# Attention backward at one query row: half of O by wide matmuls with a DRAM scratch, and sum p·dp on VectorE

## The chip, the cores and the metric

One core of one Trainium2 chip. The time is device time in microseconds (us) of one execution, and the figures are medians of several executions. The span in the profile is about 2 us shorter than the time (644.5 for 646.47 us in the profiled run of the kernel before), because it runs from the first to the last instruction.

## The reference

The reference computes softmax attention with one query row per head, and its gradients. There are 32 heads, 8192 keys and head size 128, all in bf16.

```python
scores = jnp.einsum('bhqd,bhkd->bhqk', q, k) * 128 ** -0.5     # q: 1,32,1,128   k, v: 1,32,8192,128
attn   = softmax(scores)
out    = jnp.einsum('bhqk,bhkd->bhqd', attn, v)                # out_0 = O
# out_1, out_2, out_3 = the gradients of q, k, v for grad_out (vjp)
```

For each head with p = softmax, dO = grad_out and dp = V·dO, the outputs are dV = p ⊗ dO and ds = p·(dp − sum p·dp)·scale, and from it dK = ds ⊗ q and dQ = ds·K. The sum of p·dp over the keys equals O·dO, so a kernel may take either. For each head 2 MiB each of K and V are read, and 2 MiB each of dK and dV are written: 268 MB in all.

## The kernel before

A head goes through these stages: K is transposed by blocks on VectorE, TensorE makes the scores from it, then comes the softmax. V is transposed on TensorE (32 fp32 transposes, four groups of eight). O is 64 matmuls with one moving column, each with 128 rows of V as its weights. dp comes from the transposed V, and dV and dK are outer products on VectorE. K has three buffers, V, dV and dK two each.

```python
    def contract(Xt, rep, out_col, first=0, last=NT):        # O: 64 matmuls of one column
        for n in range(first, last):
            nc.tensor.matmul(out_col, lhsT=Xt[:, n, :], rhs=rep[:, n, 0:1],
                             start=(n == 0), stop=(n == NT - 1), skip_group_check=True)
    # ... (cut) in the loop over heads, after the softmax:
        v_transposes(h, 0)
        v_transposes(h, 1)
        v_transposes(h, 2)
        contract(Vt[h], x["p"], x["m"][:, 2:3])
        nc.scalar.copy(o_all[:, h:h + 1], x["m"][:, 2:3])
        v_scores(h, 0)                                       # dp
        v_scores(h, 1)
        v_transposes(h, 3)
        nc.tensor.matmul(x["m"][:, 1:2], lhsT=do_f[:, h:h + 1].to_broadcast([P, P]),   # O.dO
                         rhs=o_all[:, h:h + 1], start=True, stop=True, skip_group_check=True)
        v_scores(h, 2)
        v_scores(h, 3)
        # ... (cut) four outer products dV, the store of dV, the load of V two heads on;
        # dK and dQ of a head follow in the next head's turn
```

## Time and profile before

| before | |
|---|---|
| time | 646.4 us (646.16 to 646.51, 3 runs) |
| DMA in mid-run | all 16 engines busy, 428 GB/s |
| TensorE, VectorE, ScalarE busy | 75%, 78%, 28% |
| mean granted TensorE clock (share of full speed that TensorE was allowed) | 0.60 |

Three more lines are wanted. The first is the page's busy times. The others are groups: busy time and mean ns of one, then idle time before them with what ended it.

```profile
PE 481.0 (75%) x9673; PEld 452.0 (70%) x9673; DVE 505.5 (78%) x653; ACT 183.5 (28%) x332; POOL 0.7 (0%) x6
...
L210 DVE TENSOR_TENSOR G_dv<-p_rep,qd 128x2048 bf16<-128x2048 bf16 x128 | 148.2, 1221 | 90.3 <-DMA out_dram<-G_dv 84.6
L183 PE MATMUL T_ps<-ident_f,Vt 128*128 128x128 f32 x1024 | 203.4, 382 | 0.2 <-PE m_ps L294 0.2
```

VectorE stands still for 84.6 us in all because an old dV has not been written out yet: compute waits for transfers. A V transpose is recorded with 382 ns on the mean of two granted clocks, 0.5 ("cold" below) and 1.0 ("warm"): it starts 213 ns after the one before at 0.5 and 109 ns after it at 1.0 (medians of this trace). The records of neighbours overlap, as their busy time of 203.4 us for 1024 (199 ns each) shows.

### The profile page before, as it was taken

To read this page: it belongs to the slowest core of one execution; us is meant where nothing else is said; L and a number is where in the kernel's file an instruction comes from. 1 tells how busy PE (TensorE), PEld (TensorE's weight loads), DVE (VectorE), ACT (ScalarE), POOL (GpSimd) and SP (SyncE) were. 2 spreads that over 40 slices of the span, in tenths; PEclk is the share of its full clock that TensorE was granted. 3 is DMA by queue.
4 is the path that set the end of the run, shared out by engine and by line. 5 is a ranking of instruction groups with operands and counts; after the bars stand their busy time and mean duration, and the time that the engine had idled before them with its cause. 6 is when DMAs were issued, how large, how long until landed. Compare 5 with 4: busy or idle time off the path is not lost.

```text
span 644.5 us, 20935 instructions
## 1 busy us (share of the span) xinstructions
PE 481.0 (75%) x9673; PEld 452.0 (70%) x9673; DVE 505.5 (78%) x653; ACT 183.5 (28%) x332; POOL 0.7 (0%) x6
## 2 busy tenths in 40 slices
PE   3898888886677877768777787667786777877780
PEld 2888888886677866768666777667785676866670
DVE  5989899867977779777788777797767977778860
ACT  2333333332233222233222332223322223222230
POOL 0000000000000000000000000000000000000000
PEclk9766666655666655666556666556655666655665
DMA  8999999999999999999999999999999999999985
GB/s 349 407 425 430 424 425 423 429 426 431 427 428 427 427 427 429 429 429 425 433 422 433 425 430 427 427 429 425 427 429 425 431 425 429 429 427 430 424 365 238
DMA packets 19718, 269.80 MB, mean 419 GB/s; under 512 B 2352, under 2 KB 2352, under 8 KB 2864
## 3 DMA queue, kind: packets, MB, share of 16 engines
q1 hardware_dynamic: 19584, 268.47, 98.2%
q8 instruction: 75, 1.23, 0.7%
q14 instruction: 11, 0.09, 0.0%
q10 hardware_dynamic: 48, 0.01, 0.0%
HBM read 134.23 MB, written 134.23 MB: 417 GB/s over the span
## 4 chain that ended last, share of the span: by engine, by line
DMA 59%; PE 21%; DVE 14%; ACT 2%; issue 1%; SPq 0%; DVEq 0%; ACTq 0%
DMA Kt<-in_k_dram 48%; DVE XK_sb L146 8%; PE T_ps L183 8%; DMA out_dram<-G_dv 5%; DMA out_dram<-G_dk 5%; PE s_ps L157 5%; DVE G_dk L210 4%; PE dp_ps L200 3%; PE m_ps L200 2%; PE dp_ps L195 2%; ACT XT_sb L185 1%; PE m_ps L294 1%; DVE G_dv L210 1%; PE s_ps L173 1%; DVE sm L163 1%
## 5 line engine op out<-in xcount | busy, mean ns | idle before, releaser
L210 DVE TENSOR_TENSOR G_dv<-p_rep,qd 128x2048 bf16<-128x2048 bf16 x128 | 148.2, 1221 | 90.3 <-DMA out_dram<-G_dv 84.6
L183 PE MATMUL T_ps<-ident_f,Vt 128*128 128x128 f32 x1024 | 203.4, 382 | 0.2 <-PE m_ps L294 0.2
L183 PEld LDWEIGHTS T_ps<-ident_f,Vt 128*128 128x128 f32 x1024 | 190.7, 210 | 0.2 <-issue 0.2
L185 ACT COPY XT_sb<-T_ps 128x1024 f32<-128x1024 f32 x128 | 128.6, 1013 | 129.3 <-PE T_ps L183 127.2
L210 DVE TENSOR_TENSOR G_dk<-ds_rep,qd 128x2048 bf16<-128x2048 bf16 x128 | 155.6, 1218 | 2.9 <-DMA out_dram<-G_dk 1.9
L146 DVE STREAM_TRANSPOSE XK_sb<-Kt 128x1024 f32<-128x1024 f32 x128 | 148.3, 1214 | 5.8 <-DMA Kt<-in_k_dram 4.7
L157 PEld LDWEIGHTS <-XK_sb 128*128 128x128 bf16 x2048 | 57.7, 104 | 90.7 <-DVE pdt L234 79.9
L157 PE MATMUL s_ps<-q_blk,XK_sb 128*128 128x4 bf16 x2048 | 59.7, 168 | 82.1 <-DVE pdt L234 72.1
L195 PE MATMUL dp_ps<-do_blk,XT_sb 128*128 128x2 bf16 x2048 | 66.7, 164 | 18.1 <-ACT XT_sb L185 18.1
L195 PEld LDWEIGHTS <-XT_sb 128*128 128x128 bf16 x2048 | 64.9, 102 | 20.7 <-ACT XT_sb L185 20.7
L200 PE MATMUL dp_ps<-ds_rep,Kt 128*128 128x1 bf16 x2048 | 64.1, 165 | 1.3 <-issue 1.0
L200 PEld LDWEIGHTS <-Kt 128*128 128x128 bf16 x2048 | 59.6, 104 | 6.8 <-issue 6.6
L244 ACT COPY dq_all<-dp_ps 128x1 f32<-128x1 f32 x32 | 5.1, 159 | 192.4 <-PE dp_ps L200 178.5
L200 PEld LDWEIGHTS <-Vt 128*128 128x128 bf16 x2048 | 57.7, 97 | 0.9
L200 PE MATMUL m_ps<-p_rep,Vt 128*128 128x1 bf16 x2048 | 56.9, 164 | 0.0
L294 PEld LDWEIGHTS m_ps<-rs,ones_f 128*128 128x128 f32 x64 | 16.0, 311 | 49.9 <-ACT e L293 49.9
L294 PE MATMUL m_ps<-rs,ones_f 128*128 128x1 f32 x64 | 18.8, 362 | 40.5 <-ACT e L293 40.5
L303 ACT ACTIVATE p_rep<-e,rinv 128x256 bf16<-128x256 f32 x32 | 16.3, 508 | 30.1 <-DVE rinv L301 30.1
L163 DVE TENSOR_TENSOR sm<-s_ps,in_quad 128x256 f32<-128x256 f32 x32 | 13.6, 424 | 11.1 <-PE s_ps L157 7.9
L229 ACT CAST qd<-s_ps 128x256 bf16<-128x256 f32 x32 | 11.9, 372 | 32.2 <-PE s_ps L225 32.2
L236 DVE SCALAR_TENSOR_TENSOR ds_rep<-dp_ps,pdt,p_s 128x256 bf16<-128x256 f32 x32 | 15.5, 484 | 5.2 <-PE dp_ps L195 2.4
L293 ACT ACTIVATE e<-s_ps,nbias 128x64 f32<-128x64 f32 x32 | 10.0, 313 | 31.8 <-DVE nbias L290 31.8
(44 smaller groups left out, 143.4 us busy)
## 6 DMA issues: line engine op xcount, KB each, us to landing
Vt<-in_v_dram SPq DMA_DIRECT2D x32, 2048.0 KB, 30.0
Kt<-in_k_dram SPq DMA_DIRECT2D x31, 2048.0 KB, 30.8
out_dram<-G_dv SPq DMA_DIRECT2D x30, 2048.0 KB, 34.6
out_dram<-G_dk SPq DMA_DIRECT2D x30, 2048.0 KB, 33.6
out_dram<-G_dv SPq DMA_DIRECT2D x4, 1024.0 KB, 15.0
out_dram<-G_dk SPq DMA_DIRECT2D x4, 1024.0 KB, 13.3
Kt<-in_k_dram SPq DMA_DIRECT2D x4, 512.0 KB, 5.1
out_dram<-fin_sb SPq DMA_DIRECT2D x2, 8.0 KB, 13.1
```

Source lines behind the costliest of these rows:

```text
L146: nc.vector.transpose(XK[h][:, :, :, u, :], slots(Kt[h], u, NCH).rearrange("p g d -> p (g d)").bitcast(F32).rearrange("p (g w j) -> p g w ...
L157: nc.tensor.matmul(out[:, g, :], lhsT=cols[:, g, c // 2, c % 2], rhs=q_blk[:, h, c, :], start=(c == 0), stop=(c == 2 * NB - 1), skip_group ...
L163: nc.vector.tensor_tensor(x["sm"][:], x["s"][:, 0:NT].rearrange("p (a g) -> p a g", a=NQ).unsqueeze(2) .to_broadcast([P, NQ, NCH, CH]), in ...
L183: nc.tensor.transpose(T_ps[:, i, :], words[:, m * P:(m + 1) * P], ident_f[:])
L185: nc.scalar.copy(X[:], T_ps[:])
L195: nc.tensor.matmul(st[h]["dp"][:, n:n + 2], lhsT=X[:, i, e2, :], rhs=do_blk[:, h, e2, :], start=(e2 == 0), stop=(e2 == 1), skip_group_chec ...
L200: nc.tensor.matmul(out_col, lhsT=Xt[:, n, :], rhs=rep[:, n, 0:1], start=(n == 0), stop=(n == NT - 1), skip_group_check=True)
L210: nc.vector.tensor_tensor(slots(G, r, 4).rearrange("p n (a b) -> p n a b", b=R), slots(rep, r, 4).unsqueeze(2).to_broadcast([P, Q, D // R, ...
L229: nc.scalar.copy(x["qd"][:].rearrange("p a d -> p (a d)"), x["s"][:, 256:512])
L236: nc.vector.scalar_tensor_tensor(out=x["ds"][:], in0=x["dp"][:, 0:NT].unsqueeze(2).to_broadcast([P, NT, R]), scalar=pdt[:], in1=x["p_s"][: ...
L294: nc.tensor.matmul(x["m"][:, 0:1], lhsT=ones_f[:], rhs=rs[:], start=True, stop=True, skip_group_check=True)
L303: nc.scalar.activation(x["p"][:], e[:].unsqueeze(2).to_broadcast([P, NT, R]), ACT.Copy, scale=rinv[:])
```

## The change

The intent is to take work off TensorE's longest stage. The first half of O is made by 8 matmuls whose *moving* operand is V, 512 columns (four rows of 128) wide, with four columns of p as weights. Of each 4x512 result only the four diagonal 1x128 blocks are wanted. The whole 8 KB go to a DRAM scratch. At the very end all diagonals are read back, summed, and added to the other half. Since O is then not known in time for O·dO, VectorE takes sum p·dp.

```diff
+    def o_wide(h):
+        for g in range(NT // 2 // R):
+            nc.tensor.matmul(x["s"][0:R, :], lhsT=x["p"][:, R * g:R * (g + 1), 0],
+                             rhs=Vt[h][:, R * g:R * (g + 1), :].rearrange("p n d -> p (n d)"),
+                             start=(g == 0), stop=(g == NT // 2 // R - 1), skip_group_check=True)
+        nc.scalar.copy(four[:], x["s"][0:R, :])
+        nc.sync.dma_start(scratch[h, 0:R * R * D].rearrange("(a c) -> a c", a=R), four[:])
+    def o_narrow(h):     # 32 one-column matmuls for the second half
+    def pd_of(h):
+        nc.vector.tensor_tensor_reduce(out=junk[:], in0=x["p_s"][:], in1=x["dp"][:, 0:NT], scale=1.0,
+                                       scalar=0.0, op0=ALU.mult, op1=ALU.add, accum_out=pd[:])
+        nc.tensor.matmul(x["m"][:, 1:2], lhsT=ones_s[:], rhs=pd[:], start=True, stop=True, ...)
 ... (cut) next head's turn, between the third and the fourth block of its K:
+        if h > 0:
+            pd_of(p_)
 ... (cut)
         v_transposes(h, 1)
+        o_wide(h)
         v_transposes(h, 2)
-        contract(Vt[h], x["p"], x["m"][:, 2:3])
-        nc.scalar.copy(o_all[:, h:h + 1], x["m"][:, 2:3])
+        o_narrow(h)
 ... (cut)
-        nc.tensor.matmul(x["m"][:, 1:2], lhsT=do_f[:, h:h + 1].to_broadcast([P, P]), rhs=o_all[:, h:h + 1], ...)
 ... (cut) last head, before the last dK:
-            result(o_all, out_0)
+            nc.sync.dma_start(blocks[:], scratch[:].rearrange("h (a c) -> h a c", a=R)[:, :, 0:D])
 ... (cut) after everything else:
+    nc.vector.reduce_sum(block_sum[:], blocks[:].rearrange("h a d -> h d a"), axis=AX.X)
+    nc.tensor.transpose(fin_ps[0:H, 0, :], o_all[:], ident_f[:])
+    nc.vector.tensor_tensor(o_sb[:], fin_ps[0:H, 0, :], block_sum[:], op=ALU.add)
+    nc.sync.dma_start(out_0.rearrange("b h s d -> (b h s) d"), o_sb[:])
```

More of the change, by code (lines that the diff above doesn't have):

```diff
@@ L54 @@
     small = ctx.enter_context(tc.tile_pool(name="small", bufs=2))
+    fours = ctx.enter_context(tc.tile_pool(name="fours", bufs=3))
+    dram = ctx.enter_context(tc.tile_pool(name="scr", bufs=1, space=bass.MemoryType.DRAM))
     psT = ctx.enter_context(tc.tile_pool(name="psT", bufs=2, space=PSUM))
@@ L122 @@
     twice = consts.tile([H, 2, 2, W], BF16)
-    do_f = consts.tile([P, H], F32)
     def do_columns():
@@ L131, in do_columns @@
             nc.tensor.transpose(tp[:, e2, 0:H], twice[:, e2].rearrange("h t j -> h (t j)"), ident[0:H, 0:H])
-        nc.tensor.transpose(tp[:, 2, 0:H], rows[:, 1, :], ident[0:H, 0:H])
         for e2 in range(2):
@@ L135, in do_columns @@
                 nc.scalar.copy(do_blk[t * W:(t + 1) * W, :, e2, t], tp[t * W:(t + 1) * W, e2, 0:H])
-        nc.scalar.copy(do_f[:], tp[:, 2, 0:H])
+    ones_s = consts.tile([P, P], F32)
+    nc.vector.memset(ones_s[:], 1.0 / scale)
+    scratch = dram.tile([H, R * (R + 1) * D], F32, name="scratch")
     o_all = consts.tile([P, H], F32)
@@ L201, in contract @@
                              start=(n == 0), stop=(n == NT - 1), skip_group_check=True)
+    def o_wide(h):
+        x = st[h]
+        for g in range(NT // 2 // R):
+            nc.tensor.matmul(x["s"][0:R, :], lhsT=x["p"][:, R * g:R * (g + 1), 0],
+                             rhs=Vt[h][:, R * g:R * (g + 1), :].rearrange("p n d -> p (n d)"),
+                             start=(g == 0), stop=(g == NT // 2 // R - 1), skip_group_check=True)
+        four = fours.tile([R, R * D], F32, tag="four", name="four")
+        nc.scalar.copy(four[:], x["s"][0:R, :])
+        nc.sync.dma_start(scratch[h, 0:R * R * D].rearrange("(a c) -> a c", a=R), four[:])
+    def o_narrow(h):
+        x = st[h]
+        for n in range(NT // 2, NT):
+            nc.tensor.matmul(x["m"][:, 2:3], lhsT=Vt[h][:, n, :], rhs=x["p"][:, n, 0:1],
+                             start=(n == NT // 2), stop=(n == NT - 1), skip_group_check=True)
+        nc.scalar.copy(o_all[:, h:h + 1], x["m"][:, 2:3])
+    def pd_of(h):
+        x = st[h]
+        junk = small.tile([P, NT], F32, tag="junk")
+        pd = small.tile([P, 1], F32, tag="pd")
+        nc.vector.tensor_tensor_reduce(out=junk[:], in0=x["p_s"][:], in1=x["dp"][:, 0:NT], scale=1.0,
+                                       scalar=0.0, op0=ALU.mult, op1=ALU.add, accum_out=pd[:])
+        nc.tensor.matmul(x["m"][:, 1:2], lhsT=ones_s[:], rhs=pd[:], start=True, stop=True, skip_group_check=True)
     def outer(h, which, r):
@@ L259 @@
             rows_bc(h)
-            for u in range(NCH):
+            for u in range(NCH - 1):
                 k_blocks(h, u)
+        if h > 0:
+            pd_of(p_)
+        if h < H:
+            k_blocks(h, NCH - 1)
             k_scores(h)
@@ L313 @@
         v_transposes(h, 3)
-        nc.tensor.matmul(x["m"][:, 1:2], lhsT=do_f[:, h:h + 1].to_broadcast([P, P]), rhs=o_all[:, h:h + 1],
-                         start=True, stop=True, skip_group_check=True)
         v_scores(h, 2)
@@ L326 @@
         if h == H - 1:
-            result(o_all, out_0)
+            blocks = consts.tile([H, R, D], F32)
+            nc.sync.dma_start(blocks[:], scratch[:].rearrange("h (a c) -> h a c", a=R)[:, :, 0:D])
     result(dq_all, out_1)
+    block_sum = consts.tile([H, D], F32)
+    nc.vector.reduce_sum(block_sum[:], blocks[:].rearrange("h a d -> h d a"), axis=AX.X)
+    fin_ps = psT.tile([P, CH // 2, P], F32, tag="T", name="fin_o")
+    nc.tensor.transpose(fin_ps[0:H, 0, :], o_all[:], ident_f[:])
+    o_sb = consts.tile([H, D], BF16)
+    nc.vector.tensor_tensor(o_sb[:], fin_ps[0:H, 0, :], block_sum[:], op=ALU.add)
+    nc.sync.dma_start(out_0.rearrange("b h s d -> (b h s) d"), o_sb[:])
     order.__exit__(None, None, None)
```

## The prediction

> **What bounds the kernel now.** I read the page from the top, then the transfers, then the chain of waits, then the timeline of two heads and of the end. First the busy slices and the rate.
>
> ```profile
> PEclk9766666655666655666556666556655666655665
> DMA  8999999999999999999999999999999999999985
> GB/s 349 407 425 430 424 425 423 429 426 431 427 428 427 427 427 429 429 429 425 433 422 433 425 430 427 427 429 425 427 429 425 431 425 429 429 427 430 424 365 238
> HBM read 134.23 MB, written 134.23 MB: 417 GB/s over the span
> ```
>
> The DMA row is full from the second slice to the last but two, at a rate that hardly moves (422 to 433 GB/s). TensorE, VectorE and ScalarE stand at 75%, 78% and 28%. The table of stretches says the same without rounding (its columns are the span of the stretch, the busy time of PE, PEld, DVE, ACT and POOL with their counts, the granted clock, the DMA share, GB/s):
>
> ```profile
> 200.00:300.00 100.00, 75.77 (x1519) 71.27 (x1519) 78.64 (x100) 28.55 (x51) 0.00 (x0) 0.59 1.01 428
> 500.00:600.00 100.00, 76.16 (x1552) 71.66 (x1551) 79.58 (x102) 28.97 (x51) 0.00 (x0) 0.59 1.01 428
> ```
>
> All 16 DMA engines are in use throughout. One head moves 4 x 2 MiB = 8.39 MB; at 428 GB/s that is 19.6 us. The chain of waits repeats with just this period:
>
> ```profile
> 234.50 30.84 DMA Kt<-in_k_dram
> 265.37 4.62 DVE XK_sb L146 x4
> 270.05 1.87 PE s_ps L157 x64
> 271.92 0.85 PE dp_ps L200 x32
> 272.77 0.37 PE s_ps L173 x8
> 273.14 0.94 PE dp_ps L200 x32
> 274.12 30.85 DMA Kt<-in_k_dram
> ```
>
> 274.12 - 234.50 = 39.62 us for two heads, 19.8 us for one. Compute is 8.8 us of it; a K tile is 30.8 us under way although 2 MiB need 4.9 us alone: some five other transfers stand ahead of it. That backlog is the slack, as a microsecond more of compute comes off the queueing, not onto the end.
>
> How close compute is to becoming the bound shows in the first 117 us, before the backlog is full: the chain there goes through compute alone, and its 24 transposes of V start at 32.89, 50.15, 67.63, 84.81 and 101.90: 17.25 us per head, 2.5 us under the transfers.
>
> The end decides what little can move:
>
> ```profile
> 626.00:630.00 4.00, 1.48 (x46) 1.21 (x43) 3.96 (x4) 0.63 (x3) 0.00 (x0) 0.50 0.80 337
> 630.00:634.00 4.00, 0.00 (x0) 0.00 (x0) 0.00 (x0) 0.00 (x0) 0.00 (x0) 0.50 0.95 398
> 634.00:638.00 4.00, 0.00 (x0) 0.00 (x0) 0.00 (x0) 0.00 (x0) 0.00 (x0) 0.50 0.57 239
> 638.00:642.00 4.00, 0.00 (x0) 0.00 (x0) 0.00 (x0) 0.00 (x0) 0.00 (x0) 0.50 0.36 152
> ```
>
> The last engine is done by 630; 12 us of writes follow, in the last 8 of which about half of the DMA engines are already idle. The packet records agree: about half finish near 634 us, the others at 640 to 643 us. So the end is the backlog of the laggards. They had some 10 us of older work when the first half of the last dK was issued at 627.7, since that dK takes them only 4.9 us. Why they lag I infer: the second line of the queues below is instruction fetch, 75 packets that share the data's engines. If they all land on eight engines, that is 75/8 x 0.61 us = 5.7 us on each, about the lag (16 KB packets take 0.61 us in the packet records).
>
> ```profile
> q1 hardware_dynamic: 19584, 268.47, 98.2%
> q8 instruction: 75, 1.23, 0.7%
> ```
>
> [...] 24 fp32 transposes take 4.7 to 5.4 us, about 0.21 us each at granted 0.5, and 8 take 0.86 us in the warm window. [...] the trace's mean of 0.59 would be 0.5 with about one window of 3.4 us in each 19.7 us.
>
> **The change part by part, per head.**
> *TensorE.* Out: 32 of the 64 V contractions (64 take 1.59 us in the chain, so -0.80) and the fp32 product of O and dO (-0.42, the two passes in the timeline). In: 8 matmuls of 512 columns, 1.7 us warm to 3.4 us cold; they follow 16 transposes that have already run 3.4 us, so I take two to four cold and the rest warm: 2.3 us. Also in: the sum of pd over the partitions, an fp32 column product of the same kind as the removed one, +0.42, but issued before the K scores, where TensorE idles (PE s_ps waited 72.1 us in all for VectorE). The last 8 transposes of V gain perhaps 0.4 us from the warmer clock. Sum: -0.80 - 0.42 + 2.3 + 0.42 - 0.4 = +1.1 us, and at worst (all cold, no gain) +2.6 us. Compute then needs 18.3 us per head, at worst 19.8, against 19.7 for the transfers. TensorE busy about 75 to 80%, mean clock 0.60 to about 0.65.
> *VectorE.* In: one reduction of 128x64 fp32 with a PSUM operand; the nearest rows are p_s (128x64, 255 ns) and mx (218 ns), so about 0.3 us with the readout of the sum. DVE has 15.8 us of work in 19.7 and waits 84.6 us in all for old dV writes: hidden.
> *ScalarE.* In: the copy of 4x512 out of PSUM. From 372 ns for 256 columns and 1013 ns for 1024 the slope is 0.83 ns, so 0.59 us, between copies that have slack (28% busy).
> *Transfers.* In: 8 KB of scratch per head and 64 KB read once: 0.33 MB of 268 MB, 0.1%. If the writes sit on four engines, each gets 2 KB per head: from 309 ns for 8 KB and 611 ns for 16 KB, 2 KB take about 0.083 us; with the semaphore write about 0.09; x 32 = 3 us on those four. If they are laggards, the end moves by 3 us; if they are of the half that is done 7 us early, by nothing. I give each half: +1.5.
> *Fewer instructions.* The build has 15,153 entries for TensorE in place of 16,660, some 190 more on the others: net some 1,300 fewer. At the fetched 1.23 MB over about 17,500 entries, 70 B each, that is 92 KB or 5.6 packets of 16 KB less: 5.6 / 8 x 0.61 = 0.4 us less on the laggards (an estimate, if eight engines do the fetching).
> *Window of transfers.* In the built order each transfer waits for the one eight before it, which shares its semaphore. A head now issues five, not four, so at most about 6.4 large ones are open where there were 6.3 to 7. I followed the order: dV of a head now waits for dK of two heads before (about 5 us later issue, landing order unchanged), the others hardly at all. Six open transfers still fill the engines: 0.
> *The end.* O's first result was written at 625.3, hidden. Now the blocks' read waits for the last scratch write, the sum comes after it, and one 8 KB write is issued last. The read stands behind the last dV, before the last dK, thus lands some 3 us before the end; sum, addition and issue fit in that or overrun: +0 to 1.5, I take +0.5. The last dK is ready about 2 us later (1.1 TensorE, 1 for pd, now serial), inside the 10 us of backlog: 0.
>
> Sum: 646.4 + 1.5 - 0.4 + 0.5 = 648.0 us.
>
> **The rivals.**
> *TensorE becomes the bound.* If the eight matmuls run cold and something adds half a microsecond, a head takes 20.3 us, and 32 x 0.5 = 16 us more: 662 us. For it: the clock, 0.5 most of the time, and only 2.5 us of distance. Against it: the warm window follows the V transposes in every head, and the 17.25 us itself held ready time on VectorE.
> *The serial end.* The blocks' read, the sum and one write after all else, each with its landing (the two small writes of before took 13.1 us behind the queue): if the last dK is held up in the issuing queue behind the wait for the last scratch write, and the read is slow, +3 to 6 us: 650 to 652.
> *Four engines hot.* All of the 3 us and a late last scratch write on laggards: 650.5.
> *Less TensorE work helps.* If the half of O and the product were on the path, -1.2 us x 32 = -38 us. The chain of waits and full DMA row speak against it: transfers alone are 627 us (268.47 MB at 428 GB/s).
>
> **Range and chances.** The floor is near 645 (less fetch, nothing else); the hot engines plus a clumsy end give 651 to 652. Range 645.0 to 652.0. 2% slower is 659.3, for which only the TensorE rival is enough: 3%. 2% faster is 633.5, at which the transfers leave 6 us for start and end: under 1%.
>
> **What would show it.** Right: DMA share 1.01 and 428 GB/s in the middle; K loads still about 30 us; a head still 19.8 us; clock up; new waits of the issuing queue on transfers, without gaps in the DMA row; the scratch writes landing late or early tells whether their engines lag. Wrong: a DMA share under 0.98 in mid-run, or VectorE waits for dV gone and TensorE waits gone (compute bound); or an end with over 3 us between the last dK and the last small write.

That no transfer time is to be won was not shown (no stretch of 100 us in the kernel before, taken from 0 to 600 us, is above 429 GB/s, but that is what it moved and not a limit). And that the scratch writes always fall on the same four engines was an assumption.

TensorE's terms can be checked in the traces. In the kernel before the clock is at 1.0 in one stretch of 3.41 us per head, which begins 2.9 to 6.0 us after the first transpose of V. In the changed kernel the 512-column matmuls start 216 ns apart at 1.0 and 426 at 0.5 (medians), so eight of them are 1.7 us warm and 3.4 cold. That two to four of the eight would be cold was an estimate; the groups of eight take 1.9 to 3.0 us in that trace's records. The last eight transposes of a head's V took 1.47 us in the mean before and 1.07 in the changed kernel, the 0.4 that the prediction took. That a scratch write has four packets of 2 KB, 84 ns each, is in the changed kernel's packet records.

## The result

The changed kernel takes 651.69 us (651.67 to 651.86, 4 runs). Beside it the kernel before took 646.28 us (646.16 to 646.51, 4 runs). The ratio is 1.0084, with a 95% interval of 1.0066 to 1.0101. A ratio here is the mean time of one kernel's fast runs over the mean of the other's fast runs of the same rounds, so it is not quite the ratio of the medians. The verdict at 2% is "same", as predicted, and the time is inside the range. But the rise is 5.4 us where the sum of the prediction had 1.6, so some terms of that sum are wrong. That the time is still inside the range is luck: its upper end, 651 to 652, was meant for hot scratch engines and a clumsy end, and neither came, as the experiments show.

The page after shows the busy times, the clock and DMA by slices, and the queues:

```profile
PE 512.7 (79%) x8904; PEld 423.2 (65%) x8904; DVE 513.0 (79%) x720; ACT 199.2 (31%) x361; POOL 0.7 (0%) x6
...
PEclk9877756677776667776567776577756777656775
DMA  8999999999999999999999999999999999999984
...
q1 hardware_dynamic: 19984, 268.80, 97.6%
q8 instruction: 69, 1.13, 0.7%
```

TensorE has 31.7 us more work, 0.99 us per head, though it runs 769 fewer matmuls. Its mean clock is 0.683. The DMA row is as full as before, and 6 packets less were fetched for instructions. The stretches in mid-run have the columns of the prediction's stretches:

```profile
200.00:300.00 100.00, 80.99 (x1403) 67.34 (x1401) 82.44 (x115) 31.49 (x59) 0.00 (x0) 0.67 1.01 426
500.00:600.00 100.00, 80.17 (x1395) 66.65 (x1394) 79.36 (x110) 30.64 (x55) 0.00 (x0) 0.67 1.01 427
```

The transfers are still saturated: share 1.01, 426 to 427 GB/s for 428. The groups that the change made or touched:

```profile
L238 DVE TENSOR_TENSOR G_dv<-p_rep,qd 128x2048 bf16<-128x2048 bf16 x128 | 148.2, 1219 | 72.1 <-DMA out_dram<-G_dv 69.1
L185 PE MATMUL T_ps<-ident_f,Vt 128*128 128x128 f32 x1024 | 183.9, 348 | 0.1
L209 PE MATMUL s_ps<-Vt,p_rep 128*4 128x512 bf16 x256 | 73.8, 441 | 0.0
L213 ACT COPY four<-s_ps 4x512 f32<-4x512 f32 x32 | 18.4, 574 | 39.2 <-PE s_ps L209 39.2
L229 PE MATMUL m_ps<-pd,ones_s 128*128 128x1 f32 x64 | 17.5, 343 | 25.0 <-DVE pd L227 24.3
```

The eight wide matmuls take 73.8 / 32 = 2.31 us per head, the predicted 2.3. V's transposes fell from 382 to 348 ns, as the clock is at 1.0 for 218 us in place of 109. VectorE still waits for old dV, 69.1 us in place of 84.6. So compute has not become the bound, but it has come nearer. The last line is new: TensorE waits for VectorE's sum, 24.3 us in all.

One longer stretch of the chain of waits shows where the two kernels differ most:

```profile
184.14 3.40 PE T_ps L185 x16
187.53 1.82 PE s_ps L209 x8
...
202.38 3.52 PE T_ps L185 x16
205.90 2.75 PE s_ps L209 x8
...
221.66 3.40 PE T_ps L185 x16
225.07 1.82 PE s_ps L209 x8
...
237.72 30.77 DMA Kt<-in_k_dram
```

Before, the first K load appeared in the chain at 117.87 us, and from then on a head took its transfers' 19.8 us. In the changed kernel the chain goes through compute alone until 237.72. Successive heads start 18.24 and 19.28 us apart. The wide group alternates between 2.75 us, at a mean clock of 0.66, and 1.82 us at 1.00.

The waits of the issuing queue (in all, times, longest) show the predicted change in the window of transfers:

```profile
SPq L248 <- DMA out_dram<-G_dk: 80.4, 20, 5.0
SPq L214 <- DMA out_dram<-G_dv: 63.7, 19, 3.7
SPq L80 <- DMA Kt<-in_k_dram: 40.4, 19, 3.1
```

These are new, and with them the DMA share in mid-run is still 1.01.

The end is where the time is lost. First the kernel before, then the changed one, in stretches of 2 us; the last two columns are the DMA share and GB/s.

```profile
639.00:641.00 2.00, 0.00 (x0) 0.00 (x0) 0.00 (x0) 0.00 (x0) 0.00 (x0) 0.50 0.40 165
641.00:643.00 2.00, 0.00 (x0) 0.00 (x0) 0.00 (x0) 0.00 (x0) 0.00 (x0) 0.50 0.09 38
643.00:644.50 1.50, 0.00 (x0) 0.00 (x0) 0.00 (x0) 0.00 (x0) 0.00 (x0) 0.50 0.00 0
```

```profile
639.00:641.00 2.00, 0.00 (x0) 0.00 (x0) 0.00 (x0) 0.00 (x0) 0.00 (x0) 0.50 0.67 270
641.00:643.00 2.00, 0.00 (x0) 0.00 (x0) 0.00 (x0) 0.00 (x0) 0.00 (x0) 0.50 0.08 31
643.00:645.00 2.00, 0.00 (x0) 0.00 (x0) 1.28 (x2) 0.00 (x0) 0.00 (x0) 0.50 0.07 29
645.00:647.00 2.00, 0.00 (x0) 0.00 (x0) 0.00 (x0) 0.00 (x0) 0.00 (x0) 0.50 0.09 33
```

From 641 to past 647 us the DMA share is 0.07 to 0.09. One engine of 16 would be 0.0625, and its part of 428 GB/s is 27. So for six microseconds the kernel waits for little more than **one** DMA engine that has fallen behind the other 15.

The trace also records when each of the 16 engines signals its part of a transfer, without the engine's number, so this can be followed through the run. The times are on the zero of the profile's views; "15th" and "last" are ranks in order of completion. I took the 112th of the 2 MiB transfers, a dV store near the end:

| engines' completion of that store, us | first | 15th | 16th (last) |
|---|---|---|---|
| before | 564.2 | 578.0 | 578.1 |
| changed | 565.0 | 577.2 | 582.6 |

The engines run apart steadily. At the third head's K load they are 2.7 us apart in the kernel before, here 14. In the kernel before several late engines end within 3 us of each other. In the changed kernel the 15th is even earlier, and one engine alone is 5.4 us behind it. It gained most of that lag between 160 and 220 us, in the prolonged compute-limited start. Its mean step from one transfer to the next tells where:

| step of the last engine, us | dV store | dK store |
|---|---|---|
| before, 120 to 240 us | 5.07 | 5.11 |
| changed, 120 to 240 us | 5.40 | 5.21 |
| before, 240 to 600 us | 5.04 | 5.04 |
| changed, 240 to 600 us | 5.00 | 5.16 |

The first engine kept 4.8 to 4.9 for all, and from 240 us on a load took the last one 4.89. So it loses on stores. In the kernel before the last place also moves on by 5.0 to 5.1 us per store, though there it changes between engines (the gap to the 15th falls back to 0.1 us several times), so part of that loss is not new; what is new lies mostly in the longer start.

### The profile page after: what moved, and what is told of

Read it like the earlier page. It is cut to its first block, busy times and chain, and to the rows that moved or that the text cites. A ratio compares the mean times of both kernels' runs of the same rounds, so it can differ in the third digit from the quotient of the medians.

```text
span 649.9 us, 19620 instructions
## 1 busy us (share of the span) xinstructions
PE 512.7 (79%) x8904; PEld 423.2 (65%) x8904; DVE 513.0 (79%) x720; ACT 199.2 (31%) x361; POOL 0.7 (0%) x6
## 4 chain that ended last, share of the span: by engine, by line
DMA 51%; PE 28%; DVE 14%; issue 4%; ACT 3%; SPq 0%; DVEq 0%; ACTq 0%
DMA Kt<-in_k_dram 39%; PE T_ps L185 10%; PE s_ps L159 6%; DVE XK_sb L148 5%; DMA out_dram<-G_dk 5%; DMA out_dram<-G_dv 5%; DVE G_dk L238 5%; PE s_ps L209 4%; PE dp_ps L197 3%; DMA blocks<-scratch 2%; PE dp_ps L202 2%; ACT XT_sb L187 2%; PE m_ps L219 1%; PE m_ps L326 1%; DVE sm L165 1%
## 5 line engine op out<-in xcount | busy, mean ns | idle before, releaser
L238 DVE TENSOR_TENSOR G_dv<-p_rep,qd 128x2048 bf16<-128x2048 bf16 x128 | 148.2, 1219 | 72.1 <-DMA out_dram<-G_dv 69.1
L185 PE MATMUL T_ps<-ident_f,Vt 128*128 128x128 f32 x1024 | 183.9, 348 | 0.1
L185 PEld LDWEIGHTS T_ps<-ident_f,Vt 128*128 128x128 f32 x1024 | 165.1, 189 | 14.5 <-issue 14.4
L159 PE MATMUL s_ps<-q_blk,XK_sb 128*128 128x4 bf16 x2048 | 59.8, 168 | 25.5 <-DVE pdt L262 18.8
L197 PEld LDWEIGHTS <-XT_sb 128*128 128x128 bf16 x2048 | 60.9, 97 | 28.1 <-ACT XT_sb L187 27.7
L209 PE MATMUL s_ps<-Vt,p_rep 128*4 128x512 bf16 x256 | 73.8, 441 | 0.0
L209 PEld LDWEIGHTS <-p_rep 128*4 128x4 bf16 x256 | 21.6, 94 | 44.8 <-issue 29.0
L326 PE MATMUL m_ps<-rs,ones_f 128*128 128x1 f32 x64 | 18.7, 360 | 40.6 <-ACT e L325 40.1
L229 PE MATMUL m_ps<-pd,ones_s 128*128 128x1 f32 x64 | 17.5, 343 | 25.0 <-DVE pd L227 24.3
L229 PEld LDWEIGHTS m_ps<-pd,ones_s 128*128 128x128 f32 x64 | 14.8, 287 | 32.6 <-DVE pd L227 32.6
L219 PEld LDWEIGHTS <-Vt 128*128 128x128 bf16 x1024 | 30.4, 96 | 0.4
L213 ACT COPY four<-s_ps 4x512 f32<-4x512 f32 x32 | 18.4, 574 | 39.2 <-PE s_ps L209 39.2
L219 PE MATMUL m_ps<-p_rep,Vt 128*128 128x1 bf16 x1024 | 30.3, 163 | 0.0
```

What stands on the lines that cost most here:

```text
L159: nc.tensor.matmul(out[:, g, :], lhsT=cols[:, g, c // 2, c % 2], rhs=q_blk[:, h, c, :], start=(c == 0), stop=(c == 2 * NB - 1), skip_group ...
L185: nc.tensor.transpose(T_ps[:, i, :], words[:, m * P:(m + 1) * P], ident_f[:])
L197: nc.tensor.matmul(st[h]["dp"][:, n:n + 2], lhsT=X[:, i, e2, :], rhs=do_blk[:, h, e2, :], start=(e2 == 0), stop=(e2 == 1), skip_group_chec ...
L209: nc.tensor.matmul(x["s"][0:R, :], lhsT=x["p"][:, R * g:R * (g + 1), 0], rhs=Vt[h][:, R * g:R * (g + 1), :].rearrange("p n d -> p (n d)"), ...
L213: nc.scalar.copy(four[:], x["s"][0:R, :])
L219: nc.tensor.matmul(x["m"][:, 2:3], lhsT=Vt[h][:, n, :], rhs=x["p"][:, n, 0:1], start=(n == NT // 2), stop=(n == NT - 1), skip_group_check= ...
```

## The experiments

The theories were these. **The scratch**: four engines get the writes and end later (the prediction's 1.5 us). **The serial end**: the read, the sum and the last write. **T, the longer compute of a head**: it lengthens the start, and one engine's stores suffer. **W, the wide matmuls' own traffic or warmth**. Unless it is said, the results were correct. Read a letter in a recorded expectation together with the paragraph ahead of it, which says what the run was to tell apart.

**The writes alone.** The kernel before, plus an 8 KB dummy write of 4 rows per head:

```diff
+        nc.sync.dma_start(scratch[h].rearrange("(a c) -> a c", a=4), filler[:])
         contract(Vt[h], x["p"], x["m"][:, 2:3])
```

> The kernel before with one dummy write per head of 8 KB from 4 partitions (2 KB each), at the place of the new scratch write; nothing reads it. Theory 1 (the four engines that carry it are among the laggards that set the end): 32 x (0.084 us packet + 0.009 us semaphore) = +3.0 us, 649.3 us. Theory 2 (a fifth transfer per head narrows the window of eight open transfers, whatever its shape): the same gain or loss as with sixteen rows. Theory 3 (the cost of the change is compute or its serial end): +0, 646.3 us.

Measured: 646.14 us beside 646.19, ratio 0.9998 (0.9986 to 1.0010). No cost of the 32 writes can be seen.

**The same bytes from 16 rows.** The edit is `a=16` in place of `a=4`, and the filler shaped to it.

> The same 8 KB per head and the same place, from 16 partitions (512 B each). Theory 1: a 512 B packet is 0.027 us, with its semaphore 0.036 us, on every engine: 32 x 0.036 = +1.2 us, 647.5 us, so clearly less than with four rows. Theory 2: as with four rows within 0.3 us. Theory 3: +0.

Measured: 647.08 beside 646.19, ratio 1.0012 (1.0000 to 1.0024). From 16 rows the writes cost 0.9 us, with an interval from 0 to 1.6. In the completion records of the dV store above, the four-row writes set four engines of the early group back by about 2 us (the 4th to 7th, 566.4 to 571.2 for 564.5 to 569.1), and these are still 6 us and more ahead of the last. That is why they are free.

**More TensorE work of the narrow kind.** The kernel before, with O's 64 one-column matmuls issued twice (second result unused):

```diff
         contract(Vt[h], x["p"], x["m"][:, 2:3])
+        contract(Vt[h], x["p"], x["m"][:, 3:4])
```

> The kernel before with the 64 contractions of V done twice per head (second sum unused): 4096 more TensorE entries, about 287 KB or 17.5 instruction packets of 16 KB more; TensorE +1.6 us per head. If the laggards lag through instruction fetch on about eight engines: 17.5/8 x 0.61 = +1.3 us; on four engines +2.7 us. If fetch has no part in the end: +0. If compute counts: it would be +0 too as long as a head needs under 19.7 us (17.25 + 1.6 = 18.9).

Measured: 670.94 beside 646.19 (668.88 to 677.2), ratio 1.0391. The chain of waits by engine of this run:

```profile
PE 71%; DVE 12%; ACT 8%; issue 6%; DMA 1%; SPq 0%; DVEq 0%; ACTq 0%
```

DMA has left the chain: this is TensorE as the bound, with a mean clock of 0.601. My expectation, at most +2.7 us, missed. A head took 20.3 us in the start and not the 18.9 of my sum: 1.6 us of added narrow work made it 3.0 us longer, with V's transposes at 402 ns for 382. 91 packets were fetched for instructions in place of 75.

**More TensorE work of the wide kind.** The kernel before, plus the change's eight wide matmuls, result unused, no scratch:

```diff
+        for g in range(NT // 2 // R):
+            nc.tensor.matmul(x["s"][0:R, :], lhsT=x["p"][:, R * g:R * (g + 1), 0],
+                             rhs=Vt[h][:, R * g:R * (g + 1), :].rearrange("p n d -> p (n d)"), ...)
         v_transposes(h, 2)
```

> The kernel before with the 8 wide matmuls added after the first 16 transposes (result unused), nothing removed: TensorE +2.0 to 2.7 us per head less what the warmer clock gives back, few more entries. Transfer-bound theory: within 0.5 us of before, granted clock up to about 0.67. Compute theory (TensorE becomes the bound): +3 us or more.

Measured: 653.26 beside 646.19 (653.07 to 653.41), ratio 1.0108 (1.0094 to 1.0121). Without any scratch, read or change of O's result the rise is 7.1 us, more than that of the whole change. DMA in mid-run stays at 427 GB/s. The end has the same shape as that of the changed kernel, again one engine's share:

```profile
643.00:645.00 2.00, 0.00 (x0) 0.00 (x0) 0.00 (x0) 0.00 (x0) 0.00 (x0) 0.50 0.06 25
645.00:647.00 2.00, 0.00 (x0) 0.00 (x0) 0.00 (x0) 0.00 (x0) 0.00 (x0) 0.50 0.07 29
647.00:649.00 2.00, 0.00 (x0) 0.00 (x0) 0.00 (x0) 0.00 (x0) 0.00 (x0) 0.50 0.07 29
```

It is also the counterpart of the run before: 2.3 us of wide work cost 7 us, 1.6 us of narrow work 25. The wide group raised the clock to 0.682 and made V's transposes shorter (348 ns, against 402 ns with the extra narrow work), so compute stayed just under the transfers (18.9 us per head in the start).

**The changed kernel without the read.** `blocks` is set to zero in place of being read (O is wrong):

```diff
-            nc.sync.dma_start(blocks[:], scratch[:].rearrange("h (a c) -> h a c", a=R)[:, :, 0:D])
+            nc.vector.memset(blocks[:], 0.0)
```

> The changed kernel without the read of the blocks from DRAM (the blocks are zeros, O is wrong on purpose); the writes, the matmuls and the last small write of O stay. Theory E (the read waits behind the queue and the sum and last write follow it: 2.6 us of the 5.4): 649.1 us. Rival (the end costs nothing, as the last dK must land anyway): 651.7 us.

Measured: 651.59 beside 646.31, ratio 1.0081 (1.0069 to 1.0094), against 1.0084 for the changed kernel. I had expected 649.1; the read costs nothing that can be seen. The sum and O's last write stay in this run. In the trace of the changed kernel that write landed at 648.5 us, 0.4 after the last dK, so little is left for them to cost.

**Nor the writes.** As the last run, and the scratch writes are removed too (O wrong).

```diff
-        nc.sync.dma_start(scratch[h, 0:R * R * D].rearrange("(a c) -> a c", a=R), four[:])
```

> As the run without the read, and without the 32 scratch writes too. After the run of four rows on the kernel before (+0.0 us) I expect nothing from this: 649.1 us, as without the read. Theory of the prediction (the four engines set the end): 3 us less than without the read.

Measured: 651.14 (650.45 to 651.39) beside 646.31, ratio 1.0073 (1.0060 to 1.0085). My 649.1 missed here too. The scratch as a whole, with its fifth transfer per head in the window, is worth some 0.5 us of the 5.4, less than the width of the intervals.

**Twice the writes.** The changed kernel with `four` written twice, 16 KB per head in one transfer; the result is correct.

```diff
-        nc.scalar.copy(four[:], x["s"][0:R, :])
-        nc.sync.dma_start(scratch[h, 0:R * R * D].rearrange("(a c) -> a c", a=R), four[:])
+        nc.scalar.copy(four[:], x["s"][0:R, :].unsqueeze(1).to_broadcast([R, 2, R * D]))
+        nc.sync.dma_start(scratch[h, :, 0:R * R * D].rearrange("t (a c) -> a t c", a=R), four[:])
```

> The changed kernel with 16 KB per head in the scratch write in place of 8 (two copies, 4 KB on each of four engines). Theory of the prediction (the four engines set the end): +2.4 us, 654.1 us. Theory that the four engines run ahead of the ones that set the end: +0, 651.7 us.

Measured: 651.97 beside 646.31, ratio 1.0088 (1.0073 to 1.0104): 0.3 us over the changed kernel, no more than the scatter between batches would explain.

**O finished early.** The last head makes all of O the narrow way, and the blocks are read and O is written before the last dK; the result is correct. It was meant as a better version.

```diff
-        o_wide(h)
+        if h < H - 1:
+            o_wide(h)
 ... (cut) the last head contracts all 64 rows; the read moves to the start of its V work,
 ... (cut) the sum and the write of O in front of its last gradients
```

> The changed kernel, correct, but the last head takes its O whole by the small matmuls, so the blocks of the other heads can be read, summed and written before the last gradients. Theory E: the serial end goes, about -2.5 us: 649.2 us. Rival: 651.7 us. If the read's wait in the issuing queue holds up the last dV: up to +2 us.

Measured: 653.46 beside 646.31, ratio 1.0111 (1.0097 to 1.0124), 1.8 us slower than the changed kernel. This is a miss. The issuing queue now stands 12.0 us before O's write, waiting on VectorE's `pd`, and holds back the last dK stores behind it. The share at the end is not that of one engine (0.97 from 645 to 647 us). Here a small result put ahead of the last large stores, and not ready in time, cost more than its landing after them.

**VectorE's sum alone.** The kernel before with `pd_of` in place of the product O·dO, O narrow as before:

```diff
+        if h > 0:
+            pd_of(p_)              # between the third and fourth block of the next K
-        nc.tensor.matmul(x["m"][:, 1:2], lhsT=do_f[:, h:h + 1].to_broadcast([P, P]), rhs=o_all[:, h:h + 1], ...)
```

> The kernel before with only the second half of the change: sum p*dp on VectorE ahead of the last K transposition of the next head, in place of the product of O and dO; O's contraction stays narrow over all of V, with no scratch. It makes the longest chain of a head neither clearly longer nor shorter. Theory T and theory W: 646.3, within 1 us. If it costs over 2 us, then VectorE's reduction is a part of the rise that neither names.

Measured: 648.73 (648.49 to 648.95) beside 646.24, ratio 1.0038 (1.0025 to 1.0051). My expectation missed: it costs 2.5 us. I had taken the longest chain of a head as unchanged. In the trace the compute-limited heads are 0.6 us longer, and the page gives the wait: TensorE stands for the new sum as it does in the changed kernel.

```profile
L208 PE MATMUL m_ps<-pd,ones_s 128*128 128x1 f32 x64 | 18.7, 361 | 44.0 <-DVE pd L206 43.7
```

The product of O and dO was ready well before dp. The sum of p·dp can only start once the last of dp is there, so it, its readout and its sum over the partitions are serial in the head. In the saturated part a head keeps its 19.9 us in spite of those waits; in the start it is longer by them.

**A delay without TensorE work.** The kernel before, plus two dummy ScalarE copies ahead of the first copy of V's transposes:

```diff
+        if c == 0:
+            for _ in range(2):
+                nc.scalar.copy(idle[:], ones_f[:, 0:1].to_broadcast([P, 1024]))
         X = tpool.tile([P, CH // 2, P], F32, tag="XT", name="XT_sb")
```

> The kernel before plus two dummy ScalarE copies (128x1024, about 1 us each) per head ahead of the first copy of V's transposes, so that the third set of transposes starts about 2 us later: a longer head without any more TensorE work. Theory T: +4 to +7 us (650 to 653), the compute-limited stretch at the start lasting to about 200 us in place of 117, with about 19.2 us per head. Theory W: within 1 us of 646.3. TensorE busy as before (481 us), ScalarE up by 65 us.

Measured: 647.93 (647.64 to 648.01) beside 646.24, ratio 1.0024 (1.0011 to 1.0038), that is 1.7 us. Neither expectation held as a number. Of the 2 us most had been slack: the compute-limited heads are only 0.6 us longer, not 2. TensorE was busy for 488 us, 7 more than before. The direction is T's: with no added matmul the time rises, and the last engine falls 1.6 us behind the 15th (table below).

**A longer delay.** Three copies in place of two.

> The kernel before plus three dummy ScalarE copies per head in place of the two of the run before, which lengthened a head in the compute-limited start from 17.25 to only 17.85 us and cost 1.7 us. The third should make it 18.8 to 18.9 us, near the 18.7 of the changed kernel, again with no TensorE work added. Theory T (what counts is the compute time of a head, thus how long the start stays limited by compute): the compute-limited start then takes 11 to 13 heads in place of 7, and the time rises by 4.5 to 6.5 us, 650.7 to 652.7; the last of the 16 engines is then 3 to 6 us behind the next in mid-run. Theory W (the wide matmuls' own traffic or the warmer clock): at most +3 us, under 649.3, the last engine at most 2 us behind the next.

Measured: 657.75 (656.63 to 658.29) beside 646.25, ratio 1.0171 (1.0157 to 1.0185): 11.5 us, outside both expectations. The third copy lengthened a head not to 18.8 but to 19.7 us. V's transposes became slower over the run (414 ns for 382 before), with the clock at 0.50 to 0.55 from 120 us on. That is not what made the start long: there the clock was 0.87 to 1.00, and a head took 19.9 us all the same. Compute is on the chain all the way:

```profile
PE 45%; ACT 29%; DVE 21%; issue 3%; DMA 1%; DVEq 0%; SPq 0%; ACTq 0%
```

Nearly all of its rise is then the pace of compute: even the first engine signals our store at 573.7 us, 9.5 later than before. The dose that would have matched the changed kernel was not hit, so this run does not decide between T and W. One thing it does show: its last engine is 5.7 us behind the 15th without a single wide matmul, and from 240 to 600 us it steps by 5.36 us per dV store and 5.16 per dK store.

**The wide matmuls with four rows.** The eight wide matmuls added to the kernel before, contracting 4 partitions in place of 128:

```diff
-            nc.tensor.matmul(x["s"][0:R, :], lhsT=x["p"][:, R * g:R * (g + 1), 0], rhs=Vt[h][:, ...
+            nc.tensor.matmul(x["s"][0:R, :], lhsT=x["p"][0:R, R * g:R * (g + 1), 0], rhs=Vt[h][0:R, ...
```

> The kernel before plus eight matmuls of 512 columns per head whose result is not used, as in the earlier experiment that took +7.1 us, but each contracts 4 partitions in place of 128: the same columns and so the same TensorE time, with 1/32 of the moving data read from SBUF. Theory T (the longer compute per head is what costs): +5 to +8 us, 652 to 654. Theory W (the traffic of the wide operand[...] slows the transfers): at most +2 us, under 648.5. TensorE busy some 35 us over the kernel before under both, clock 0.65 to 0.70.

Measured: 682.66 (681.4 to 686.18) beside 646.24, ratio 1.0574. This is far outside both expectations, and the page says why:

```profile
PEclk9986556665555665556566556656555655565655
...
PE 72%; DVE 14%; ACT 8%; issue 2%; DMA 1%; DVEq 0%; SPq 0%; ACTq 0%
...
L183 PE MATMUL T_ps<-ident_f,Vt 128*128 128x128 f32 x1024 | 224.3, 401 | 0.0
```

The clock was warm for less of the time. In mid-run it is 0.55, where the 128-row version has 0.67, though TensorE was busier (86% against 81% of the span). The eight matmuls take 3.50 us, cold throughout, in 13 of 32 heads, and 1.81 to 2.2 in the others (with 128 rows the warm groups take 1.82), V's transposes take 401 ns in place of 348, and a head takes 19.2 to 22 us in all but the first and one other. So it could not serve as the test of traffic that I had meant it for. But it shows the prediction's rival, TensorE as the bound, as it would have come: same columns, as many instructions, a colder clock, and 36 us more.

## Why the prediction was right or wrong

The runs that stayed saturated nearly line up when sorted by the compute time of a head in the start (the mean of the second to sixth distance between first K transposes). The last three columns are the completions of the store used above.

| kernel | head in the start | heads before the first distance over 20 us | rise of time | first | 15th | 16th |
|---|---|---|---|---|---|---|
| before | 17.2 us | 7 | – | 564.2 | 578.0 | 578.1 |
| before, four-row writes | 17.2 | 7 | 0.0 | 563.8 | 577.5 | 577.7 |
| before, sixteen-row writes | 17.1 | 7 | +0.9 | 565.1 | 578.6 | 579.0 |
| VectorE's sum alone | 17.8 | 8 | +2.5 | 564.4 | 578.7 | 580.4 |
| delay of two copies | 17.8 | 8 | +1.7 | 563.8 | 578.2 | 579.7 |
| changed, no scratch | 18.7 | 12 | +4.8 | 564.2 | 577.5 | 582.2 |
| changed | 18.7 | 11 | +5.4 | 565.0 | 577.2 | 582.6 |
| changed, twice the writes | 18.7 | 12 | +5.7 | 565.5 | 577.5 | 583.0 |
| changed, no read | 18.9 | 13 | +5.3 | 564.9 | 577.6 | 582.7 |
| wide matmuls alone | 18.9 | 13 | +7.1 | 564.1 | 578.2 | 584.3 |

The first engine and the 15th hardly move. Where compute was lengthened, the 16th moves by 1.6 to 6.2 us, and the time by about the same. In this group the end of the kernel is the end of one DMA engine. The line is not strict: without the read a head is as long as with the wide matmuls alone, and the rise is 1.8 us smaller. So the head's length does not seem to fix the rise by itself, though 18.7 and 18.9 for the change with and without the read, which have the same start, show how far this measure scatters. Nor does the lag grow without end: in the two runs bound by TensorE (narrow work doubled, wide matmuls with four rows) the last engine is only 0.6 and 0.8 us behind the 15th.

Point by point:

- **The bound.** Right. The transfers set the pace (share 1.01), the K loads are still 30.8 us under way, a head takes 19.9 to 20.0 us in mid-run for 19.8. The reading that the end is the backlog of laggards is right too. One detail of the reading was loose: the second slice has 407 GB/s, outside its "422 to 433".
- **"Compute ... a microsecond more comes off the queueing, not onto the end": the step that failed.** It is the TensorE term, set to 0 in the sum. Its work was sized well: +0.99 us per head for +1.1, the wide group 2.31 for 2.3, a head of 18.7 us for 18.3. But its cost at the end is about 5 us, not 0 (worked out as the rise of 5.4 less some 0.5 for the scratch). The wide matmuls alone give +7.1. The mean engine does have the slack that I read from the backlog. The last engine has none, and in the saturated runs it lost more where compute was longer. The prediction's signs of being right all came (share 1.01, K loads of 30.8 us, a warmer clock), since they look at the mean engine; none of them could show this.
- **"The last dK is ready about 2 us later ... 0", with the serial pd in it.** The same step on a smaller scale: the sum on VectorE alone costs 2.5 us.
- **Scratch on four engines, +1.5.** Too high: the writes alone 0.0, the whole scratch some 0.5. The coin fell on the early engines. My inference that the lag is instruction fetch was half right: it fits the group of late engines, not the last one.
- **Fetch, −0.4.** The count was right (75 to 69 packets for 5.6 fewer; the pages list 20935 and 19620 instructions, 1315 fewer). The size per packet was not: an engine's step of about 4.9 us becomes 6.3 to 6.4 where a fetch falls, so a packet costs 1.4 to 1.5 us and not 0.61. The packet's own record is 1.0 us. On eight engines 75 packets of 1.45 us are 13.6 us, an estimate beside the 13.9 that the engines are apart in the kernel before. The eight are half of the 16, as in the prediction; of that store's completions seven came by 569.1 us and nine from 575.5 on. The 15th engine's gain fits too (577.2 for 578.0), but in the changed kernel the last place shows no such step after 120 us.
- **The serial end, +0.5.** 0.1 without the read, inside the scatter. Its parts came as described: the read landed at 643.2 us, the sum took 1.02 us, and O's write was issued at 644.6, before the last dK landed at 648.1.
- **The window of eight, 0.** The transfers do use eight semaphores in turn (17 or 18 each in the trace of before). The waits came and no gap followed; its cost is within the 0.5 of the scratch.

In place of 1.5 − 0.4 + 0.5 the runs put about 5 from the longer compute and some 0.5 from the scratch. The parts don't add up linearly: wide alone +7.1 and the sum alone +2.5 make 9.6, so taking away half of the narrow matmuls and the product would have to be worth some −4. That is worked out by difference and was not run alone.

What stays open: why that one engine loses on its stores, and which of the 16 it is, as the records have no number. Two additions with no wide matmul, the delay and VectorE's sum, shift it by 1.6 and 2.3 us for 0.6 us more per head. That supports T at that dose, and the longer delay shows as large a lag as the changed kernel's without any wide matmul. But it overshot in time, the four-row run changed the clock, and at equal heads the wide matmuls alone cost 1.8 us more than the change without the read, so a share of W, the wide operand's own traffic or warmth, is not excluded. No version tried beats the kernel before.

**What the traces show of the clock.** The clock records of both traces hold two levels, 1.0 and 0.5. From about 20 us on, where the records begin, the clock is at 1.0 in 32 stretches, one per head: of 3.41 us each in the kernel before (109 us in all), of 6.83 us each in the changed one (218 us). So the prediction's "one window of 3.4 us in each 19.7 us" is what the kernel before had. The stretch is not tied to one place in a head: it begins 2.9 to 6.0 us after the first transpose of V before, and 2.9 to 5.8 us after it in the changed kernel. That is the alternation of 1.82 and 2.75 us for the same eight matmuls, and it goes with that of 18.2 and 19.3 us for heads. What starts a stretch, and what made it longer, was not shown. The wide matmuls follow the clock: 438 ns each in the cold groups of 3.50 us (the four-row run), 226 to 228 in the warm ones of 1.81 and 1.82.

## What to carry to other kernels

This kernel, bound by transfers, ended with its slowest DMA engine and not with the mean one: a full DMA row and a backlog of 10 us did not make extra compute free. Read the end in stretches of 2 us; a share near 1/16 can be one engine, and the completion records tell. And if added matmuls are to stay hidden, ask what they do to TensorE's clock before counting their columns: here 2.3 us of full-row matmuls cost 7 us, and the same columns with four rows cost 36.
